# First weight loads as two half-megabyte transfers, layer-norm moments on ScalarE, and earlier row gathers, in a kernel bound by TensorE

## The chip, the cores and the metric

The kernel runs on one core of a Trainium2 chip. The metric is the device time of one execution in microseconds (us). On most chips the executions of one kernel agree within about 0.3%, with single ones about 1% off, so differences of 0.3% can be seen only with several runs of both kernels, taken on the same chip in alternating rounds. All runs told of here are undisturbed ("fast"). Every ratio is the mean time of one kernel's fast runs over the mean time of the kernel before in the same rounds, with a 95% interval; it is therefore not quite the ratio of the medians that stand beside it. "Same" means within 2%.

Engine names: PE is TensorE's matmuls, PEld its weight loads, DVE is VectorE, ACT is ScalarE, POOL is GpSimd, SP is SyncE, which here only issues transfers. All times inside a trace count from the start of the profiled span.

## The reference

The input x is 2048 rows of 512, in bfloat16. It is layer-normalized; one branch filters it in the frequency domain, the other is a gated MLP; the output is the sum of x and both branches.

```python
xn = _layernorm(x, axis=-1)                         # (1, 2048, 512)
# A: 2-D real FFT, times (w_r + 1j*w_i), inverse FFT
# B: with w_gate, w_up (512 x 1792) and w_down (1792 x 512)
g = jnp.einsum("bsd,df->bsf", xn, w_gate)
u = jnp.einsum("bsd,df->bsf", xn, w_up)
b = jnp.einsum("bsf,fd->bsd", gelu(g) * u, w_down)
return x + A(xn) + b
```

## The kernel before

A small list scheduler written into the kernel orders all operations; each has an engine, a duration, its dependencies and a priority. The rows of x are cut into 16 "columns" of 128 rows. The first four columns are transposed on TensorE, so that the gate and up matmuls can begin as soon as column 0 is normalized and the first slices of the weights are there. Later columns are transposed by transfers.

The loads, in the order of issue. The first two slices (128 columns each) of gate go on SP's queue, those of up on ScalarE's queue:

```python
    load_x(0, 1)                              # 128 KB
    d_ident = load_ct("ident", "ident", "ACT")
    load_x(1, 1)
    load_w(0, 2, ("SP", "ACT"))               # gate 256 KB on SP, up 256 KB on ScalarE's queue
    ...                                       # (a dummy GELU: loads ScalarE's table)
    load_x(2, 2)
    load_w(2, 4)
    load_w(4, 6)
    load_x(4, 4)
    load_w(6, 10)
    load_x(8, 4)
    load_w(10, 14)
```

Column 0 is transposed in two halves that share one PSUM buffer (the other columns in one piece); ScalarE copies the first half out, VectorE the second:

```python
    def pe_transpose(c, due):
        b = _Buf("S")                         # one buffer for the column
        ...
            o = pe(0.24 / n, mm, (XN[c][h], d_ident), due - 2, new=(b,) if h == 0 else (), use=(b,))
            XT[c].append((act, dve)[h](0.1 + 0.35 / n, ev, (o,), due - 30, use=(b,)))
```

The first matmul groups take column 0 alone, then column 1 alone, then pairs; and the six row gathers of the spectral weights wait for column 11 to be normalized:

```python
    FIRST = [(0, 1, 0, 4), (1, 1, 0, 4), (0, 2, 4, 2), (2, 2, 0, 2), (2, 2, 2, 2), (2, 2, 4, 2)]
    ...
    d_tw.append(dma(P * n * 2, lambda ...: gather(k, s, c, a, n), [g_idx] + XN[11], 20, eng="POOL", issue=1.2))
```

## Time and profile before

| what | before |
|---|---|
| time | 179.41 us (median of 3), later 179.33 (6 runs) |
| span of the profiled run | 177.6 us |
| TensorE busy | 173.4 us, 98% |
| first transpose | 5.78 us |
| first gate matmul | 6.89 us |
| first group of 512-wide gate matmuls (full pace) | 18.52 us |
| last matmul | 174.70 us |

The page of the kernel before, its busy times by engine and the chain of waits that ended last:

```profile
PE 173.4 (98%) x1100; PEld 92.9 (52%) x1100; DVE 118.1 (66%) x266; ACT 87.4 (49%) x158; POOL 18.6 (10%) x33
PE 91%; ACT 3%; DVE 3%; issue 1%; POOL 0%; DVEq 0%; POOLq 0%
```

TensorE is the bound. From 18.52 us to the last matmul it hardly waits; a change of the kind studied here can only shift that block to the left, by doing the first 18 us in less time. The timeline of PE in the kernel before; the columns are start, duration, engine, line, operation, output <- inputs, shape and count:

```profile
5.78 0.65 PE L428 MATMUL tp<-CT,xn 128*128 128x128 bf16 x4
6.23 0.63 PE L380 MATMUL warm<-warm 128*128 128x128 bf16 x4
6.89 0.82 PE L502 MATMUL g_ps<-xnT,Wg_sb 128*128 128x128 bf16 x8
7.55 0.61 PE L502 MATMUL u_ps<-xnT,Wu_sb 128*128 128x128 bf16 x8
...
18.52 1.03 PE L502 MATMUL g_ps<-xnT,Wg_sb 128*128 128x512 bf16 x4
```

`tp` are the transposes of column 0, `warm` are fillers, meant only to keep TensorE's clock up, `g_ps` and `u_ps` are gate and up. The first useful gate matmul comes 1.1 us after the first transpose. It needs the first half of column 0, which ScalarE copies from 6.47 to 6.84; VectorE's copy of the second half starts only after that, and holds up the third matmul. The timelines of ACT and DVE in the kernel before show both copies (the last column says what the engine sat idle for):

```profile
6.47 0.37 ACT L431 COPY xnT<-tp 128x256 bf16<-128x256 bf16 x1 [3.29 <-PE tp L428]
6.88 0.29 DVE L431 COPY xnT<-tp 128x256 bf16<-128x256 bf16 x1 [0.83 <-ACT xnT L431]
```

The view of the transfers issued in the first 2.5 us of the kernel before (queue, count, size of each, us from issue to landing): gate, issued at 1.65 us, lands at 5.85; up, issued at 1.12 on ScalarE's queue, at about 5.3.

```profile
Wu_sb<-in_B_w_up_dram ACTq DMA_DIRECT2D x1, 256.0 KB, 4.2
Wg_sb<-in_B_w_gate_dram SPq DMA_DIRECT2D x1, 256.0 KB, 4.2
```

### The profile page before, as it was taken

Reading aid. Unit: us, or ns where it says so; the run is one execution under the profiler, and the core shown is the slowest. Engines: PE = TensorE matmul, PEld = TensorE weight load, DVE = VectorE, ACT = ScalarE, POOL = GpSimd, SP = SyncE. Lnnn points to the kernel's source line nnn. Section 1 sums busy time; section 2 is a strip of 40 time slices with the busy share of each in tenths; the row PEclk is TensorE's granted clock in tenths of the full one; section 3 lists DMA queues with packets and bytes.
Section 4 is the critical chain, followed back from the end, with each engine's and each line's share of the span. In section 5 each row is a group of like instructions: output and inputs, shape, how many; then the busy total and the mean of one; then the engine's idle time right before and its main releaser. Section 6 shows DMA issues by size and latency. Waiting matters only on the chain.

```text
span 177.6 us, 3041 instructions
## 1 busy us (share of the span) xinstructions
PE 173.4 (98%) x1100; PEld 92.9 (52%) x1100; DVE 118.1 (66%) x266; ACT 87.4 (49%) x158; POOL 18.6 (10%) x33
## 2 busy tenths in 40 slices
PE   6999999999999999999999999999999999999993
PEld 2598545545554544554555455554445444544463
DVE  1869999999537995889999885336442541632522
ACT  3162437456789737999998855453111211211100
POOL 3212138743200000000000000000000000000000
PEclk9999999999999999999999999999999999999999
DMA  5999487999297001302211121100222221322212
GB/s 144 311 355 359 86 270 84 223 296 193 52 347 255 2 0 29 93 2 59 61 48 37 37 59 37 27 0 0 84 68 66 83 89 59 92 80 69 74 45 59
DMA packets 23182, 19.24 MB, mean 108 GB/s; under 512 B 8512, under 2 KB 21824, under 8 KB 23168
## 3 DMA queue, kind: packets, MB, share of 16 engines
q1 hardware_dynamic: 22176, 17.57, 35.0%
q0 software_dynamic: 320, 1.19, 3.1%
q10 hardware_dynamic: 672, 0.30, 0.6%
q8 instruction: 8, 0.13, 0.3%
q14 instruction: 6, 0.05, 0.1%
HBM read 13.28 MB, written 2.10 MB: 87 GB/s over the span
## 4 chain that ended last, share of the span: by engine, by line
PE 91%; ACT 3%; DVE 3%; issue 1%; POOL 0%; DVEq 0%; POOLq 0%
PE u_ps L502 25%; PE g_ps L502 25%; PE warm L380 3%; ACT E L652 2%; PE yp L818 2%; PE bp L581 2%; PE gp L767 2%; PE yp__2078 L872 2%; PE yp__1994 L872 2%; PE yp__1967 L872 2%; PE yp__1936 L872 2%; PE yp__1909 L872 2%; PE yp__1820 L872 2%; PE yp__1793 L872 2%; PE yp__1762 L872 2%; PE yp__1735 L872 2%
## 5 line engine op out<-in xcount | busy, mean ns | idle before, releaser
L502 PE MATMUL g_ps<-xnT,Wg_sb 128*128 128x512 bf16 (+2 forms) x264 | 58.1, 347 | 0.0
L502 PE MATMUL u_ps<-xnT,Wu_sb 128*128 128x512 bf16 (+2 forms) x264 | 57.9, 347 | 0.0
L527 DVE TENSOR_TENSOR hT<-u_ps,ge 128x512 bf16<-128x512 f32 x56 | 38.4, 685 | 17.5 <-PE u_ps L502 14.4
L519 ACT ACTIVATE ge<-g_ps 128x512 bf16<-128x512 f32 x56 | 33.5, 598 | 30.5 <-PE g_ps L502 26.5
L502 PEld LDWEIGHTS <-Wu_sb 128*128 128x128 bf16 x264 | 24.3, 98 | 22.3 <-DMA Wu_sb<-in_B_w_up_dram 0.2
L502 PEld LDWEIGHTS <-Wg_sb 128*128 128x128 bf16 x264 | 24.3, 98 | 20.7 <-issue 0.2
L872 PEld LDWEIGHTS <-hT 128*128 128x128 bf16 x252 | 23.0, 98 | 21.9
L824 ACT CAST yf<-yp 128x512 bf16<-128x512 f32 x16 | 9.3, 586 | 37.6 <-PE yp L818 37.6
L652 ACT CAST E<-ep 64x512 bf16<-64x512 f32 x32 | 18.5, 579 | 1.1 <-PE ep L646 0.7
L396 DVE BATCH_NORM_STATS2 st<-x_t 128x6 f32<-128x512 bf16 x16 | 10.5, 676 | 4.8 <-DMA x_t<-in_A_x_dram 4.8
L629 ACT CAST ds<-dp 128x512 bf16<-128x512 f32 x16 | 8.8, 589 | 1.1 <-PE dp L624 1.0
L773 ACT CAST Gs<-gp 128x512 bf16<-128x512 f32 x16 | 8.6, 593 | 1.0 <-PE gp L767 1.0
L406 POOL TENSOR_TENSOR rstd<-ve,half 128x2 f32<-128x2 f32 (+2 forms) x7 | 6.6, 949 | 21.9 <-DVE ve L404 21.9
L585 ACT CAST Bs<-bp 128x512 bf16<-128x512 f32 x16 | 8.3, 603 | 0.5 <-PE bp L581 0.5
L818 PEld LDWEIGHTS <-Gs 128*128 128x128 bf16 x64 | 4.8, 98 | 3.5
L380 PE MATMUL warm<-warm 128*128 128x512 bf16 (+1 forms) x14 | 5.1, 539 | 1.3 <-POOL half L373 1.3
L412 DVE TENSOR_SCALAR xn<-x_t,mv,rstd 128x512 bf16<-128x512 bf16 (+1 forms) x17 | 6.1, 399 | 0.3 <-POOL rstd L406 0.3
L818 PE MATMUL yp<-CT,Gs 128*128 128x128 bf16 x64 | 6.0, 219 | 0.0
L683 DVE TENSOR_TENSOR m<-X,TW 128x1024 bf16<-128x1024 bf16 x8 | 5.5, 692 | 0.2
L624 PEld LDWEIGHTS <-Bs 128*128 128x128 bf16 x64 | 4.4, 98 | 2.4
L689 DVE TENSOR_TENSOR m<-X,TW 128x1024 bf16<-128x1024 bf16 x8 | 5.5, 684 | 0.0
L646 PE MATMUL ep<-ds,CT 128*128 128x512 bf16 x16 | 5.4, 379 | 0.0
(103 smaller groups left out, 169.0 us busy)
## 6 DMA issues: line engine op xcount, KB each, us to landing
y<-in_A_x_dram SPq DMA_DIRECT2D x16, 128.0 KB, 2.1
F<-F SPq DMA_DIRECT2D x32, 64.0 KB, 2.0
out_dram<-y SPq DMA_DIRECT2D x15, 128.0 KB, 1.7
Wd_sb<-in_B_w_down_dram SPq DMA_DIRECT2D x2, 896.0 KB, 8.3
x_t<-in_A_x_dram SPq DMA_DIRECT2D x3, 512.0 KB, 6.8
Wg_sb<-in_B_w_gate_dram SPq DMA_DIRECT2D x2, 512.0 KB, 6.8
Wu_sb<-in_B_w_up_dram SPq DMA_DIRECT2D x2, 512.0 KB, 9.1
Wg_sb<-in_B_w_gate_dram SPq DMA_DIRECT2D x3, 256.0 KB, 5.1
```

The source lines that it names most:

```text
L380: nc.tensor.matmul(tiles["warm"][:, 0:w], lhsT=warm[:, 0:P], rhs=warm[:, 0:w], start=True, stop=True)
L396: V.bn_stats(out=st[:], in_=x_t[:, c])
L502: nc.tensor.matmul(tiles[f"{nm}.{key}"][:, f * w:f * w + w], lhsT=W[:, e, (f0 + f) * P:(f0 + f + 1) * P], rhs=rhs(e), start=(f + e == 0), ...
L519: nc.scalar.activation(out=e[:, 0:nf * w], in_=tiles[f"g_ps.{key}"][:, 0:nf * w], func=AF.Gelu_apprx_tanh)
L527: V.tensor_tensor(out=out, in0=tiles[f"u_ps.{key}"][:, 0:nf * w].rearrange("p (f w) -> p f w", w=w) if nf > 1 else tiles[f"u_ps.{key}"][:, ...
L585: nc.scalar.copy(out=o, in_=tiles[f"bp.{cg}.{q}"][:].rearrange("p c (r g a) -> p (c r) g a", r=2, a=4))
L629: nc.scalar.copy(out=ds[:].rearrange("p (s k t) -> p s k t", s=2, t=2), in_=tiles[f"dp.{G}"][:].rearrange("p s t k -> p s k t"))
L652: nc.scalar.copy(out=tiles[f"E.{g}"][64 * h:64 * h + 64, r], in_=tiles[f"ep.{g}.{h}"][64 * r:64 * r + 64])
L773: nc.scalar.copy(out=o, in_=tiles[f"gp.{g}.{h}"][:].rearrange("p q (n a) -> p (q n) a", a=4))
L818: nc.tensor.matmul(yp[:, q], lhsT=tiles["G"][:, q, c], rhs=IQ[q], start=(q == 0), stop=(q == 3), skip_group_check=True)
L824: nc.scalar.copy(out=tiles[f"yf.{c // 2}"][:, c % 2], in_=tiles[f"yp.{c}"][:])
L872: nc.tensor.matmul(y[:, s], lhsT=tiles[sb, f][:, cl * P:(cl + 1) * P], rhs=Wd_sb[:, f, s], start=(f == 0), stop=False)
```

## The change

The intent: the first weights come as two loads of four slices, gate then up, both on SP's queue, with rows of 1 KB instead of 512 B; ScalarE computes mean and variance of columns 1 and 3, so that column 1 is ready sooner and VectorE has less to do; each transposed half has a PSUM buffer of its own; the matmuls of a group use the first half of the contraction first; columns 2 and 3 go one by one; the gathers wait for column 3 only and so run between the weight loads. The core of the diff:

```diff
-    load_w(0, 2, ("SP", "ACT"))
+    load_w(0, 4)
     load_x(2, 2)
-    load_w(2, 4)
     load_w(4, 6)
...
+    def layernorm_act(c, due, halves, after=(), after2=()):
+        ...
+        s = act(0.62, lambda: moment(AF.Identity, scale=-1.0 / D, accum_out=sm[:, k:k + 1]), ...)
+        q = act(0.72, lambda: moment(AF.Square, bias=sm[:, k:k + 1], scale=1.0, accum_out=sm[:, k + 1:k + 2]), ...)
...
     def pe_transpose(c, due):
-        b = _Buf("S")
...
         for h in range(n):
+            b = _Buf("S")
...
-    layernorm(1, 1, -25, first)
...
+    layernorm_act(1, -25, 2)
...
+    layernorm(2, 1, -22, XN[1])
...
+    layernorm_act(3, -19, 1, XT[0], XT[1])
...
-                            [g_idx] + XN[11], 20, eng="POOL", issue=1.2))
+                            [g_idx] + XN[3], 20, eng="POOL", issue=1.2))
...
-            for f in range(a, b):
-                for e in range(NE):
+            for f, e in sorted(((f, e) for f in range(a, b) for e in range(NE)), key=lambda k: (k[1] // 2, k)):
...
-        step = min(nf, 2)
+        step = 4 if n == 1 else min(nf, 2)
...
-    FIRST = [(0, 1, 0, 4), (1, 1, 0, 4), (0, 2, 4, 2), (2, 2, 0, 2), (2, 2, 2, 2), (2, 2, 4, 2)]
+    FIRST = [(0, 1, 0, 4), (1, 1, 0, 4), (0, 2, 4, 2), (2, 1, 0, 4), (3, 1, 0, 4), (2, 2, 4, 2)]
```

The rest of the diff adjusts durations and delays that the scheduler believes, makes the statistics of columns 4 to 15 wait for column 3, and cuts the fillers after the first transposes from four to two.

The scheduler plans with the loads and the gathers, so an edit of either can also change the order of instructions on the engines.

More of the change, by code (lines that the diff above doesn't have):

```diff
@@ L172, in run @@
                         continue
-                    at = max([d.end + d.lag + self.HOP for d in o.deps if d.eng != "PE" or o.eng != "PE"] + [0.0])
+                    at = max([d.end + (0.0 if d.eng == o.eng and not d.nbytes else d.lag + self.HOP)
+                              for d in o.deps if d.eng != "PE" or o.eng != "PE"] + [0.0])
                     if o.nbytes and o.eng != "POOL" and len(lanes) >= 8:
@@ L265 @@
     eps = pc.tile([P, 2], F32, name="eps")
+    sm = pc.tile([P, 4], F32, name="sm")
     tiles = {}
@@ L314, in load_x @@
         q = nc.sync if eng == "SP" else nc.scalar
-        o = load(n * P * D * 2, lambda: q.dma_start(out=x_t[:, c0:c0 + n], in_=x_v[:, c0:c0 + n]), deps, eng=eng)
+        o = load(n * P * D * (1.9 if c0 > 1 else 1), lambda: q.dma_start(out=x_t[:, c0:c0 + n], in_=x_v[:, c0:c0 + n]), deps, eng=eng)
         for c in range(c0, c0 + n):
@@ L323, in load_w @@
             q = nc.sync if e == "SP" else nc.scalar
-            os.append(load(NE * P * P * 2 * (f1 - f0),
+            os.append(load(NE * P * P * (2.3 if f1 - f0 < 4 else 2.05) * (f1 - f0),
                            lambda t=t, v=v, q=q: q.dma_start(out=t[:, :, a:b], in_=v[:, :, a:b]), eng=e))
@@ L374 @@
     wb = _Buf("S")
-    NWARM, NGAP, GAP = 10, 1, 4
+    NWARM, NGAP, GAP = 10, 1, 2
     def warm_mm(w):
@@ L405, in layernorm, with moment, normalize @@
             out=ve[:, k], in0=mv[:, k, 1], scalar1=EPS, scalar2=None, op0=ALU.add), ag, due - 5)
+        normalize(c0, n, due, e, halves)
+    def layernorm_act(c, due, halves, after=(), after2=()):
+        k = 2 * (c // 2)
+        def moment(func, **kw):
+            nc.scalar.activation(out=xn[:, c], in_=x_t[:, c], func=func, **kw)
+        s = act(0.62, lambda: moment(AF.Identity, scale=-1.0 / D, accum_out=sm[:, k:k + 1]), [XD[c]] + list(after), due - 30)
+        q = act(0.72, lambda: moment(AF.Square, bias=sm[:, k:k + 1], scale=1.0, accum_out=sm[:, k + 1:k + 2]), [s] + list(after2), due - 30)
+        e = dve(0.07, lambda: V.tensor_scalar(
+            out=ve[:, c:c + 1], in0=sm[:, k + 1:k + 2], scalar1=1.0 / D, scalar2=EPS, op0=ALU.mult, op1=ALU.add), (q,), due - 9)
+        normalize(c, 1, due, e, halves, sm[:, k:k + 1], ALU.add)
+    def normalize(c0, n, due, e, halves, mean=None, op=ALU.subtract):
+        k = slice(c0, c0 + n)
         r = add("POOL", 0.55, lambda: nc.gpsimd.tensor_tensor(
@@ L412, in layernorm, with ev @@
                 XN[c].append(dve(0.04 + 0.29 / halves, lambda c=c, d=d: V.tensor_scalar(
-                    out=xn[:, c, d], in0=x_t[:, c, d], scalar1=mv[:, c, 0:1], scalar2=rstd[:, c:c + 1],
-                    op0=ALU.subtract, op1=ALU.mult), (r,), due - 2.5))
-        return ag
+                    out=xn[:, c, d], in0=x_t[:, c, d], scalar1=mv[:, c, 0:1] if mean is None else mean,
+                    scalar2=rstd[:, c:c + 1], op0=op, op1=ALU.mult), (r,), due - 2.5))
     def pe_transpose(c, due):
         XT[c] = []
-        b = _Buf("S")
         n = len(XN[c])
         for h in range(n):
+            b = _Buf("S")
             es = range(h * NE // n, (h + 1) * NE // n)
             def mm(h=h, es=es):
-                if h == 0:
-                    psum(f"tp.{c}", [P, NE, P], BF16)
+                psum(f"tp.{c}.{h}", [P, NE, P], BF16)
                 for e in es:
-                    nc.tensor.transpose(tiles[f"tp.{c}"][:, e], xn[:, c, e * P:(e + 1) * P], ident)
-            def ev(es=es, eng=(nc.scalar.copy, V.tensor_copy)[h]):
-                eng(out=xnT[c // 4][:, es[0]:es[-1] + 1, c % 4], in_=tiles[f"tp.{c}"][:, es[0]:es[-1] + 1])
-            o = pe(0.24 / n, mm, (XN[c][h], d_ident), due - 2, new=(b,) if h == 0 else (), use=(b,))
+                    nc.tensor.transpose(tiles[f"tp.{c}.{h}"][:, e], xn[:, c, e * P:(e + 1) * P], ident)
+            def ev(h=h, es=es, eng=(nc.scalar.copy, V.tensor_copy)[h]):
+                eng(out=xnT[c // 4][:, es[0]:es[-1] + 1, c % 4], in_=tiles[f"tp.{c}.{h}"][:, es[0]:es[-1] + 1])
+            o = pe(0.24 / n, mm, (XN[c][h], d_ident), due - 2, new=(b,))
             XT[c].append((act, dve)[h](0.1 + 0.35 / n, ev, (o,), due - 30, use=(b,)))
@@ L438, in dma_transpose @@
                     XN[c], due - 30, lag=1.0)]
-    first = layernorm(0, 1, -28, (), 2)
-    layernorm(1, 1, -25, first)
-    for c in range(4):
-        if c == 2:
-            layernorm(2, 2, -22, XT[0])
-        pe_transpose(c, -28 + 3 * c)
-        if c < NGAP:
-            dummies(GAP, -29.9 + 3 * c, XN[c], P)
+    layernorm(0, 1, -28, (), 2)
+    layernorm_act(1, -25, 2)
+    pe_transpose(0, -28)
+    dummies(GAP, -29.9, XN[0], P)
+    pe_transpose(1, -25)
+    layernorm(2, 1, -22, XN[1])
+    pe_transpose(2, -22)
+    layernorm_act(3, -19, 1, XT[0], XT[1])
+    pe_transpose(3, -19)
     for c0, n, due in ((4, 2, 14), (6, 2, 16), (8, 4, 24), (12, 4, 32)):
-        layernorm(c0, n, due)
+        layernorm(c0, n, due, XN[3])
         for c in range(c0, c0 + n):
@@ L499, in mm @@
                 psum(f"{nm}.{key}", [P, D], tag=tag)
-            for f in range(a, b):
-                for e in range(NE):
-                    nc.tensor.matmul(tiles[f"{nm}.{key}"][:, f * w:f * w + w], lhsT=W[:, e, (f0 + f) * P:(f0 + f + 1) * P],
-                                     rhs=rhs(e), start=(f + e == 0), stop=(f == nf - 1 and e == NE - 1),
-                                     skip_group_check=nf > 1)
+            for f, e in sorted(((f, e) for f in range(a, b) for e in range(NE)), key=lambda k: (k[1] // 2, k)):
+                nc.tensor.matmul(tiles[f"{nm}.{key}"][:, f * w:f * w + w], lhsT=W[:, e, (f0 + f) * P:(f0 + f + 1) * P],
+                                 rhs=rhs(e), start=(f + e == 0), stop=(f == nf - 1 and e == NE - 1),
+                                 skip_group_check=nf > 1)
         g = [o for c in range(c0, c0 + n) for o in XT[c]]
-        step = min(nf, 2)
+        step = 4 if n == 1 else min(nf, 2)
         us = []
```

## The prediction

> **What bounds the kernel now.** The page gives TensorE 98% of the span, and the chain of waits is TensorE for 91% of it. From 11.70 us to 174.93 us the chain is matmuls at full pace (0.86 us for four 128x512); the waits view shows no TensorE wait after the first loads. So only the start can give time.
>
> In the chain and timeline, warm-up matmuls fill 1.34 to 5.79. The first transpose (column 0) waits until 5.78 for the normalized half; the first gate matmul comes at 6.89. From there to 11.70 the useful work is 64 matmuls of 128 columns and 12 transposes: 76 x 0.056 = 4.23 us. Lost there, from the single matmul records: 0.21 us after the second gate matmul (the second half of column 0 is not yet copied; the VectorE copy starts at 6.88, only after the ScalarE copy that ran 6.47 to 6.84), and 0.17 us before 8.84 (PEld waits for Wu_sb). Between 5.79 and 6.89 four transposes and four fillers run at half pace (107 ns each).
>
> **What the change does.**
> - A PSUM buffer per transposed half: the ScalarE copy can start about 6.2 instead of 6.47, the VectorE copy about 6.47. The gate matmuls take all slices of half one first, so they can start near 6.6 and not stop for half two. Saves about 0.3 and 0.2 us.
> - Weights: kilobyte packets take 46 ns, 512 B packets 27 ns in the trace, so a megabyte takes about 3.0 us instead of 3.5. Gate (four slices) should land near 5.2 to 6, up near 6.7 to 7.4, needed only at 7.5. Saves 0.17 us.
> - Column 1 on ScalarE: the Trainium skill ("ScalarE: Activation LUTs", "What ACT_TABLE_LOAD costs") gives 186 ns + 0.833 ns per element, 93 ns more per pointer operand: estimate 0.61 and 0.71 us; the trace agrees roughly (copies of 128x512: 0.59). Moments done near 5.3, its transposes come near 6.5 instead of 8.0, partly in dead time: 0 to 0.2 us saved.
> - Columns 2 and 3 go separately, in 64 narrow matmuls instead of 32 of 256 columns: adds 0.07 us.
> - Row gathers (1.19 MB, six of 1 to 1.7 us on GpSimd) move from 27-36 us to about 11-18, among the weight loads, and delay rstd of columns 4 to 7. Weights 6 to 9 land near 14.5, needed near 18; columns 4 to 7 have about 7 us to spare. Off the chain: 0.
>
> The clock: the Trainium skill ("TensorE: Matmul & The Clock Gate", "Part 1: The HAM clock gate") says the array starts at half rate and is released after a busy window of 3413 ns, at a moment the kernel does not set. The trace agrees: 427 ns between dummies, 107 between fillers up to 6.55, 56 from 6.89 on. Work brought before about 6.8 runs at half pace, which takes back about 0.1 us.
>
> **Sum.** 0.3 + 0.2 + 0.17 + 0.1 - 0.07 - 0.1 = about 0.6 us of 179.4: predicted 178.8 us, range 178.1 to 179.5. Chances: faster by over 2%: 0.01; within 2%: 0.98; slower: 0.01.
>
> **What would show it.** First gate matmul near 6.6, no gap after it; the first 128x512 gate group about 18.0 instead of 18.5; from there the same chain, shifted by 0.6 us; gathers at 11 to 18 us with no TensorE wait.
>
> **What would make it wrong.** The up weights land later than 7.5, since they queue behind 0.5 MB of gate; gathers slow x or weight loads so that TensorE waits near 10 to 20 us; the clock is released a window later (up to 1.7 us worse); ScalarE's moments hold up the copy of column 0; the new instruction order makes new stalls in the middle, which has none now.

## The result and the profile after

The kernel after took 179.86 us (median of 6 runs, 179.59 to 180.43), the kernel before in the same rounds 179.33 (6 runs, 179.21 to 179.73). The ratio is 1.0032, interval 1.0011 to 1.0053. The class is "same", as predicted, but the sign is wrong: a loss of about 0.5 us instead of a gain of 0.6, and outside the predicted range.

The page of the kernel after, busy times by engine and chain of waits:

```profile
PE 171.7 (96%) x1112; PEld 92.8 (52%) x1130; DVE 118.5 (66%) x265; ACT 90.1 (51%) x166; POOL 17.1 (10%) x34
PE 93%; DMA 4%; issue 1%; SPq 1%; DVE 0%
```

A transfer is in the chain now, 4% of a span of 178.2 us. (PE's busy time is not to be compared closely: 1112 matmuls are recorded against 1130 weight loads, so some matmul records are missing, and regular gaps of 0.22 us in this trace are such holes.) The timeline of PE in the kernel after (its last line counts one matmul because the view's window ended at 19.2 us):

```profile
5.49 0.54 PE L443 MATMUL tp<-CT,xn 128*128 128x128 bf16 x4
5.87 0.28 PE L381 MATMUL warm<-warm 128*128 128x128 bf16 x2
7.29 1.07 PE L517 MATMUL g_ps<-xnT,Wg_sb 128*128 128x128 bf16 x16 [1.14 <-DMA Wg_sb<-in_B_w_gate_dram]
8.19 0.39 PE L443 MATMUL tp<-CT,xn 128*128 128x128 bf16 x4
8.80 1.07 PE L517 MATMUL u_ps<-xnT,Wu_sb 128*128 128x128 bf16 x16 [0.22 <-DMA Wu_sb<-in_B_w_up_dram]
...
19.00 0.38 PE L517 MATMUL g_ps<-xnT,Wg_sb 128*128 128x512 bf16 x1
```

The first transposes are 0.3 us earlier than before, yet the first gate matmul is 0.4 us later, because TensorE stands 1.14 us for the gate weights, and again for up. The first 512-wide group comes at 19.00 instead of 18.52; from there to the last matmul it is 156.14 us against 156.18. The whole loss of the profiled run that can be placed, 0.48 of 0.6 us, is in the first 19 us. The waits view of the kernel after (engine, output, line <- releaser: us in total, times, longest us), of which the kernel before has only one line of this kind, 0.2 us of PEld for up:

```profile
PEld L517 <- DMA Wg_sb<-in_B_w_gate_dram: 1.3, 1, 1.3
PE g_ps L517 <- DMA Wg_sb<-in_B_w_gate_dram: 1.1, 1, 1.1
PEld L517 <- DMA Wu_sb<-in_B_w_up_dram: 0.4, 1, 0.4
PE u_ps L517 <- DMA Wu_sb<-in_B_w_up_dram: 0.2, 1, 0.2
```

PEld and PE are two sides of one wait, not two. The view of the transfers issued in the first 2.5 us of the kernel after:

```profile
Wg_sb<-in_B_w_gate_dram SPq DMA_DIRECT2D x1, 512.0 KB, 5.6
Wu_sb<-in_B_w_up_dram SPq DMA_DIRECT2D x1, 512.0 KB, 6.6
```

Gate was issued at 1.65 us, as before, and landed at 7.25; up, issued at 2.12, landed at 8.75. The prediction had said 5.2 to 6 and 6.7 to 7.4. The chain in order of time of the kernel after begins, after the issue of the loads on SP, with just this transfer:

```profile
2.12 6.63 DMA Wu_sb<-in_B_w_up_dram
8.75 0.05 issue
8.80 1.07 PE u_ps L517 x16
```

What the change meant to do inside the core worked. The timelines of ACT and DVE in the kernel after show ScalarE's moments of column 1 and the two copies of column 0, which no longer wait for each other:

```profile
3.53 0.63 ACT L413 ACTIVATE xn<-x_t 128x512 bf16<-128x512 bf16 x1 [0.92 <-DMA x_t<-in_A_x_dram]
4.07 0.19 ACT L413 ACTIVATION_READ_ACCUMULATOR xn<-x_t 128x1 f32 x1
4.29 0.72 ACT L413 ACTIVATE xn<-x_t,sm 128x512 bf16<-128x512 bf16 x1
5.81 0.37 ACT L446 COPY xnT<-tp 128x256 bf16<-128x256 bf16 x1 [0.71 <-PE tp L443]
6.07 0.29 DVE L446 COPY xnT<-tp 128x256 bf16<-128x256 bf16 x1 [0.32 <-PE tp L443]
```

Both halves were copied by 6.36, so the gate matmuls could have begun near 6.3.

### Why the gate weights were late

The table counts the packets of 512 B or more that start on each queue in a quarter of a microsecond, from the packet records of the traces. Queue SP carries x and then gate; after its last packets of x (1 KB each) there is a stretch with almost nothing on it.

| us | before: SP / ScalarE | after: SP | gate on ScalarE's queue (a3 below): SP / ScalarE |
|---|---|---|---|
| 2.90 to 3.15 | 20 / 33 | 35 | 40 / 9 |
| 3.15 to 3.40 | 20 / 68 | 11 | 13 / 26 |
| 3.40 to 3.65 | 5 / 123 | 11 | 5 / 48 |
| 3.65 to 3.90 | 3 / 138 | 5 | 0 / 80 |
| 3.90 to 4.15 | 66 / 81 | 37 | 0 / 87 |
| 4.15 to 4.40 | 95 / 40 | 57 | 0 / 93 |

SP's third load, then, starts to flow only near 3.9 us in the kernel before too. But there the packets of up on ScalarE's queue fill that stretch; in the kernel after nothing does. In addition, seven 1 KB packets of SP's queue that start between 2.9 and 4 us in the kernel after take 0.5 to 1.29 us each, where such a packet usually takes 0.046. And a load is done only when all its parts are. The Trainium skill ("DMA: Bandwidth & Descriptors", "Why a DMA increments its semaphore by 16 and not by 1") says that each of the 16 DMA engines posts its own increment; the trace agrees, with 16 records of 4 bytes for each load. In the kernel after, 15 of gate's had been written by 5.86 us and the 16th not before 6.49. From the last such record to the landing it is some 0.4 us more (in run d4 below, 5.87 and 1.65 + 4.6 = 6.25). Run d4 also shows which of these matters more: there SP's queue had started its first 768 packets of 1 KB (256 of x and as many as gate has) at 5.34 us, against 5.50 in the kernel after, but the last part of gate was written at 5.87, against 6.49 or later. Most of the 1.0 us between these two landings is thus the last part, and not the stretch.

How full the transfer engines were can be read too. By the view of stretches of time the core moved, between 2.90 and 4.00 us, 64 GB/s in the kernel after, 242 in the kernel before and 238 in a3; between 4.00 and 7.20 it moved 351, 306 and 339 GB/s, with the 16 engines busy all the time. So the rate is no limit in the stretch, but it is one after it.

### The profile page after: what moved, and what is told of

Its sections match the earlier page's. It is cut to its first block, busy times and chain, and to the rows that moved or that the text cites. A ratio compares the mean times of both kernels' runs of the same rounds, so it can differ in the third digit from the quotient of the medians.

```text
span 178.2 us, 3088 instructions
## 1 busy us (share of the span) xinstructions
PE 171.7 (96%) x1112; PEld 92.8 (52%) x1130; DVE 118.5 (66%) x265; ACT 90.1 (51%) x166; POOL 17.1 (10%) x34
## 4 chain that ended last, share of the span: by engine, by line
PE 93%; DMA 4%; issue 1%; SPq 1%; DVE 0%
PE u_ps L517 27%; PE g_ps L517 26%; DMA Wu_sb<-in_B_w_up_dram 4%; PE bp L596 2%; PE gp L782 2%; PE yp L833 2%; PE dp L639 2%; PE ep L661 2%; PE yp__2111 L887 2%; PE yp__1969 L887 2%; PE yp__1911 L887 2%; PE yp__1826 L887 2%; PE yp__1795 L887 2%; PE yp__1739 L887 2%; PE yp__2058 L887 2%; PE yp__2027 L887 2%
## 5 line engine op out<-in xcount | busy, mean ns | idle before, releaser
L517 PE MATMUL u_ps<-xnT,Wu_sb 128*128 128x512 bf16 (+2 forms) x276 | 57.3, 336 | 0.5 <-DMA Wu_sb<-in_B_w_up_dram 0.2
L517 PE MATMUL g_ps<-xnT,Wg_sb 128*128 128x512 bf16 (+2 forms) x272 | 56.4, 335 | 1.4 <-DMA Wg_sb<-in_B_w_gate_dram 1.1
L667 ACT CAST E<-ep 64x512 bf16<-64x512 f32 x32 | 18.5, 579 | 1.8 <-PE ep L661 1.4
L397 DVE BATCH_NORM_STATS2 st<-x_t 128x6 f32<-128x512 bf16 x14 | 9.4, 673 | 3.8 <-DMA x_t<-in_A_x_dram 3.8
L423 POOL TENSOR_TENSOR rstd<-ve,half 128x1 f32<-128x1 f32 (+2 forms) x8 | 6.4, 809 | 23.9 <-DVE ve L405 23.1
L429 DVE TENSOR_SCALAR xn<-x_t,mv,rstd 128x512 bf16<-128x512 bf16 (+1 forms) x15 | 5.4, 406 | 1.6 <-POOL rstd L423 1.6
L381 PE MATMUL warm<-warm 128*128 128x512 bf16 (+1 forms) x12 | 4.4, 533 | 1.3 <-POOL half L374 1.3
L782 PEld LDWEIGHTS <-F 128*128 128x128 bf16 x64 | 4.2, 98 | 1.9
```

The source lines that it names most:

```text
L397: V.bn_stats(out=st[:], in_=x_t[:, c])
L517: nc.tensor.matmul(tiles[f"{nm}.{key}"][:, f * w:f * w + w], lhsT=W[:, e, (f0 + f) * P:(f0 + f + 1) * P], rhs=rhs(e), start=(f + e == 0), ...
L667: nc.scalar.copy(out=tiles[f"E.{g}"][64 * h:64 * h + 64, r], in_=tiles[f"ep.{g}.{h}"][64 * r:64 * r + 64])
```

## The experiments

The theory: the new order and size of the first loads costs the time, and the rest of the change gains. Its rivals: the gathers among the weight loads cost it, or ScalarE's moments and the new order of the instructions do. Eighteen runs were made: eleven new kernels, six of these or the kernel after once more, and the kernel of a6 under the name d4. Each gave the reference's result.

### a1 and a2: the loads alone, undone and done

a1 is the kernel after with the loads and the `step` of before:

```diff
-    load_w(0, 4)
+    load_w(0, 2, ("SP", "ACT"))
     load_x(2, 2)
+    load_w(2, 4)
...
-        step = 4 if n == 1 else min(nf, 2)
+        step = min(nf, 2)
```

> The changed kernel with the first weights loaded as before (two slices in 512-byte rows, the first up slices on the other queue, the next two slices after x) and the gate and up matmuls again two slices at a time; all the rest of the change stays. Theory L (the loss is the late landing of the first four-slice gate and up loads: 7.2 and 8.75 us): first gate matmul near 6.3 to 6.6 us, no TensorE wait over 0.3 us after it, total 178.7 to 179.0, faster than before by 0.2 to 0.4%. Rival R (the loss is from the gathers, the ScalarE moments or the new instruction order): 179.7 to 180.0, slower than before as the changed kernel is.

a2 is the kernel before with only the loads of after (the reverse edit, without the change of `step`).

> The kernel before with only the new loads (gate then up, four slices each, on one queue). Theory L: the first gate matmul waits for the weights until 7.0 to 7.4 and the up matmul until about 8.7, total 179.9 to 180.6. Rival R: within 0.15% of before, 179.1 to 179.6.

Before took 179.31 (11 runs). a1 took 178.98, ratio 0.9991 (0.9950 to 1.0031; one of its six runs at 181.0 widens it): no wait for weights, and these two lines in its timeline of PE:

```profile
6.74 0.61 PE L518 MATMUL g_ps<-xnT,Wg_sb 128*128 128x128 bf16 x8
18.36 1.03 PE L518 MATMUL g_ps<-xnT,Wg_sb 128*128 128x512 bf16 x3
```

So gate was used at 6.74, and the first 512-wide group came at 18.36. a2 took 181.22, ratio 1.0108 (1.0088 to 1.0128), clearly slower. The edit of the loads alone cost the kernel before 1.9 us, more than a2's expectation had (179.9 to 180.6) and more than the whole change lost. The waits view of a2 shows why it is more:

```profile
PE g_ps L501 <- ACT xnT L430: 0.8, 1, 0.8
PEld L501 <- DMA Wu_sb<-in_B_w_up_dram: 0.6, 1, 0.6
PE u_ps L501 <- DMA Wu_sb<-in_B_w_up_dram: 0.5, 1, 0.5
```

Beside the wait for up there is one, at 14.9 us, for the transposed columns 2 and 3. Their x, issued at 2.69 behind the megabyte of weights, was waited for until 8.67. What held them after that is in a2's chain: the scheduler, planning with the new loads, had put VectorE's statistics of column 4 before the normalization of columns 2 and 3, and these stood until 11.65 for the x of columns 4 to 7, issued at 4.68. So a part of the 1.9 us is this new order. Gate itself was not late in a2: its first gate matmul came at 6.68, where 7.0 to 7.4 had been expected. In a1 too the order changed on VectorE and ScalarE, and `step` with it. a3, below, is the clean test: it moves one load and leaves the order on every compute engine as it was.

### a3 and a4: one of the two loads on ScalarE's queue

The order of all instructions is kept; only the first gate load (a3) or the first up load (a4) is issued on ScalarE's queue right after the identity matrix, at 1.12 us.

```diff
-    load_w(0, 4)
+    load_w(0, 4, ("ACT", "SP"))        # a4: ("SP", "ACT")
...
     order = plan.run()
+    order.remove(WD[0][0])             # a4: WD[0][1]
+    order.insert(order.index(d_ident) + 1, WD[0][0])
```

> The changed kernel, same instruction order on every compute engine, but the four-slice gate load is issued on the ScalarE queue right after ident (about 1.1 us); up stays on the first queue. Theory L, with the cause that 3.0 to 4.0 us is a hole in the transfers because nothing else is in flight while the gate load starts up: gate lands near 5.3 to 6.0, up near 7.0 to 7.6, first gate matmul near 6.4, total 178.6 to 179.0. If the four-slice loads are slow as such (kilobyte rows or size, whatever the queue): gate still lands near 7, total 179.6 to 180.0. Rival R: unchanged, 179.7 to 180.0.

> The changed kernel, same order, but the four-slice up load is on the ScalarE queue (as in the kernel before) and gate on the first. Theory L: up fills the hole and lands near 5.5 to 6.5, but gate shares the engines with it and lands near 7 to 7.5: the first gate matmul comes no earlier than 6.9, the wait for up (8.75) is gone; total 179.2 to 179.6, between the changed kernel and a3. Rival R: unchanged, 179.7 to 180.0.

a3 took 179.28, ratio 0.9990 (0.9965 to 1.0015); a4 179.50, ratio 1.0003 (0.9986 to 1.0021). The first gate matmul and the transfer of up in a3, from its timeline of PE and its view of transfers:

```profile
6.77 1.22 PE L517 MATMUL g_ps<-xnT,Wg_sb 128*128 128x128 bf16 x16
Wu_sb<-in_B_w_up_dram SPq DMA_DIRECT2D x1, 512.0 KB, 5.6
```

In a3 gate landed at 1.12 + 4.7 = 5.8 us, and there is no wait for weights at all; the first 512-wide group came at 18.29, against 19.00. (The time is nevertheless above the expected 178.6 to 179.0; in this trace column 0 was ready late, with the first transpose at 5.91.) Up, now SP's third load, took the 5.6 us that gate had taken. In a4 gate took 5.6 again, though the other 512 KB had left its queue, and the wait of 0.9 us stayed:

```profile
7.28 1.07 PE L517 MATMUL g_ps<-xnT,Wg_sb 128*128 128x128 bf16 x16 [0.92 <-DMA Wg_sb<-in_B_w_gate_dram]
```

So in both kernels the load on ScalarE's queue landed at 5.7 to 5.8 and the one on SP's queue, behind x, at 7.25. This doesn't separate the place on the queue from the bytes that go before: in a4 the core moved 374 GB/s between 4.00 and 4.60 us with all 16 engines busy, nearly all of it up, and SP's third load began only at 4.60. In a4 up was there early (5.7), which took the second wait away, and the 512-wide group came at 18.60.

The Trainium skill ("DMA: Bandwidth & Descriptors", "Rules for kernel authors") says that spreading transfers over issuing engines doesn't help bandwidth and only saves issue time. Here gate landed 1.43 us sooner (7.25 to 5.8); 0.53 of that is the earlier issue (1.65 to 1.12), the other 0.9 is a shorter time from issue to landing. In this stretch, where SP's queue started few packets, the second queue gave more than issue time: 238 GB/s instead of 64 between 2.90 and 4.00 us.

### b1, b2, a5, a6: on a chip where the kernel before varied more

These four ran together on a chip where the kernel before took 180.03 (179.45 to 181.77), a wide spread. b1 splits the first gate and up loads into two halves of the contraction, which is what the first matmuls use first; b2 does the same and puts gate's first half on ScalarE's queue.

```diff
+            for h in range(2 if f0 == 0 else 1):
+                q = nc.scalar if f0 + h == 0 and t is Wg_sb else nc.sync      # b2 only
+                es = slice(2 * h, 2 * h + 2) if f0 == 0 else slice(0, NE)
-                           lambda t=t, v=v, q=q: q.dma_start(out=t[:, :, a:b], in_=v[:, :, a:b]), eng=e))
+                               lambda ...: q.dma_start(out=t[:, es, a:b], in_=v[:, es, a:b]), eng="SP"))
...
+    order.remove(WD[0][2])                                                    # b2 only
+    order.insert(order.index(d_ident) + 1, WD[0][2])
```

> The changed kernel, same instruction order on every compute engine and same queue, but the first gate and up loads are each cut in two loads of 256 KB by the contraction halves (still kilobyte rows), which is the order in which the matmuls use them. If size is the cause (a matmul that needs 256 KB waits for a 512 KB load): the first half lands near 6.0 to 6.3, the first gate matmul comes at 6.2 to 6.5, up near 8.0 to 8.3, total 179.0 to 179.4. If the slow start of the load after x on this queue is the cause, whatever its size: first gate matmul still after 6.8, total 179.5 to 180.0.

> As b1, with the first gate half on the ScalarE queue right after ident (256 KB there, as much as the kernel before had of up). Theory L: it lands near 5.3, the first gate matmul waits for column 0 only (6.3 to 6.8), the rest of gate lands by 7.0 and up by 8.0 with no TensorE wait over 0.2 us; total 178.5 to 178.9, faster than before by 0.2 to 0.45%. Rival R: 179.6 to 180.0.

a5 is a1 with the moments of columns 1 and 3 back on VectorE:

```diff
-    layernorm_act(1, -25, 2)
+    layernorm(1, 1, -25, (), 2)
-    layernorm_act(3, -19, 1, XT[0], XT[1])
+    layernorm(3, 1, -19, XT[1])
```

> The kernel of a1 (old loads, which take the late weights away) with columns 1 and 3 normalized from VectorE statistics again. If the ScalarE moments gain what was forecast (0 to 0.2 us): first 128x512 gate group 0 to 0.2 us later than in a1 (18.36), total 178.9 to 179.2. If they hurt: earlier than in a1, total under 178.8.

a6 is the kernel after with the gathers late, as before:

```diff
-                            [g_idx] + XN[3], 20, eng="POOL", issue=1.2))
+                            [g_idx] + XN[11], 20, eng="POOL", issue=1.2))
```

> The changed kernel with the row gathers after column 11 again, as before; same order on TensorE and ScalarE. Theory L: no effect on the critical path, total within 0.15% of the changed kernel (179.6 to 180.1), first gate matmul still near 7.2, up near 8.7. Rival R (gathers among the weight loads cost the time): 179.3 or less.

b1 took 181.80, ratio 1.0075; b2 180.92, 1.0033 (0.9989 to 1.0077); a5 180.88, 1.0034 (0.9992 to 1.0077); a6 181.25, 1.0058 (1.0016 to 1.0099). In their first 19 us b1, b2 and a6 did what was hoped: b1's gate matmuls began at 6.46, b2's at 6.24, and the 512-wide group came at 18.45 and 18.26; a6 still waited 0.7 us for gate and came to it at 18.42. a5's profiled run, the longest of its seven (182.99), came to that group only at 21.44, after a row of waits from 17 us on. In the others the time was lost later, in waits of 0.6 to 1.5 us between 18 and 36 us, of which another chip showed the like only in c3 and c4 (0.7 and 0.97, below). In a6, TensorE waited 1.5 us at 34.3 for VectorE, which itself stood still for 1.47 us with no wait for x. I don't know what this chip did there. The call decides nothing on sizes below 1%, and so b2, a1, a5 and the kernel after were run once more elsewhere.

### c1 to c4: the same kernels once more

c1 is the kernel after, c2 is a1, c3 is a5, c4 is b2, all unchanged. Before took 179.40 (179.16 to 179.59).

> The changed kernel itself, so that the three others of this call have it on the same chip. Theory L: 0.1 to 0.5% slower than before; gate load landing 5.2 to 5.7 us after its issue, up 6.3 to 6.8 after its issue, first 128x512 gate group 18.4 to 19.0. The last call ran on a chip whose kernel before was slower and more spread (180.03, 179.45 to 181.77), and its waits from 19 to 36 us are not understood; if this call runs on such a chip, the same waits should show in all four.

> The kernel of a1 (old loads, all the rest changed). Theory L: 0.4 to 0.8 us faster than c1; against before 0.1 to 0.4% faster. Rival R: equal to c1 within 0.2 us.

> The kernel of a5 (old loads, columns 1 and 3 from VectorE statistics). If the ScalarE moments are worth what was forecast: 0 to 0.2 us slower than c2. If they cost: faster than c2 by over 0.1 us.

> The kernel of b2 (first gate half on the ScalarE queue). Theory L: first 128x512 gate group 18.1 to 18.3, fastest of the four: 0.5 to 1.0 us faster than c1, 0.2 to 0.45% faster than before. Rival R: equal to c1 within 0.2 us.

c1 took 179.94, ratio 1.0026 (1.0013 to 1.0039): the loss of the kernel after is real. Its waits view repeats the cause:

```profile
PE g_ps L517 <- DMA Wg_sb<-in_B_w_gate_dram: 1.2, 1, 1.2
PE u_ps L517 <- DMA Wu_sb<-in_B_w_up_dram: 0.2, 1, 0.2
```

Gate again took 5.6 us to land, and the 512-wide group came at 19.04. c2 took 179.15, ratio 0.9987 (0.9968 to 1.0006); c3 179.38, 0.9996 (0.9983 to 1.0009); c4 179.37, 0.9997 (0.9974 to 1.0019). ScalarE's moments are thus worth 0.2 us at most in the medians, and the intervals of c2 and c3 overlap: no effect can be claimed.

c2, c3 and c4 came to the 512-wide group at 18.33, 18.16 and 18.12, earlier than the 18.52 of before, but their profiled runs were the longest of each (180.02, 179.89 and 180.29) and lost it again. The timeline of DVE in c2:

```profile
19.66 0.69 DVE L398 BATCH_NORM_STATS2 st<-x_t 128x6 f32<-128x512 bf16 x1 [1.22 <-DMA x_t<-in_A_x_dram]
```

The x of columns 8 to 11, issued at 8.2 us, landed at 19.65, against 17.3 in the kernel before and 18.5 in a1's good trace. VectorE has almost no idle time in c2 from 14 to 45 us except this, so it is late for the folds of the spectral branch, and TensorE waits for those: 0.28, 0.36 and 0.37 us between 27.7 and 42.6 us. c4 showed the same with columns 12 to 15 (landing 30.8 us, VectorE idle for 1.1 us, a TensorE gap of 0.97 us at 34.2). That the landing of x decides this is read from the traces; that the early gathers make it late was still only a theory.

### d1 to d4: the gathers

d1 is a1, d2 is b2, d4 is the kernel after, each with late gathers (the edit of a6). d3 is the opposite: the kernel before with early gathers and no other edit. In d2 and d4 only GpSimd's own order changes with it; in d1 and d3 the scheduler also moved a few of VectorE's instructions (some eight of 266 in d3).

```diff
-                            [g_idx] + XN[11], 20, eng="POOL", issue=1.2))
+                            [g_idx] + XN[3], 20, eng="POOL", issue=1.2))
```

> The kernel of a1 (old loads) with the row gathers after column 11 again, as in the kernel before. Theory G (the early gathers delay x of columns 8 to 15, VectorE, which is busy without a break from 14 to 45 us, waits for them and hands the delay to TensorE's fold matmuls): x of columns 8 to 11 lands by 17.8 (18.5 in a1, 19.65 in its repeat), no VectorE wait for x after 12 us, no TensorE wait over 0.3 us from 20 to 50, total 178.5 to 178.9 in every run, spread under 0.5 us. Rival N (the waits from 20 to 50 us are chip noise or come from the new instruction order): spread as in a1 and its repeat (178.5 to 181.0).

> The kernel of b2 (first gate half on the ScalarE queue) with late gathers. Theory G: first 128x512 gate group 18.1 to 18.3 and no later waits over 0.3 us: 178.4 to 178.8, faster than before by 0.3 to 0.5%. Rival N: 178.8 to 180.3 as in its repeat.

> The kernel before with the early gathers alone (order on TensorE and ScalarE the same as before). Theory G: x of columns 8 to 11 lands 1 to 2 us later than the 17.3 of before, VectorE waits for it in some runs, total 179.4 to 180.4 with a spread over 0.5 us. Rival N: as before, 179.2 to 179.6.

> The changed kernel with late gathers (a6 again, on this call's chip). Its start is as late as the changed kernel's (gate and up waits stay, first 128x512 gate group near 19.0), so with either theory 179.6 to 180.0; with theory G no VectorE wait for x after 14 us.

Before took 179.43 (179.01 to 180.12). d3 took 180.32, ratio 1.0056 (1.0028 to 1.0083): the early gathers, with the order that the scheduler then made, cost the kernel before about 0.9 us. Its profiled run, at 179.88 one of the faster ones, shows the gathers between 9.8 and 19.7 us instead of 27.4 to 35.6, and these waits, the second in place of 4.8 us in two waits before:

```profile
PEld L502 <- DMA Wu_sb<-in_B_w_up_dram: 0.5, 1, 0.5
DVE st L396 <- DMA x_t<-in_A_x_dram: 5.2, 3, 3.3
```

The 512-wide group is at 18.65 and the time from there to the last matmul 156.55, 0.37 more than before. The wait for up, at 8.97 us, comes before the first gather (9.84), so it can't be put down to the gathers; the later part can, or to VectorE's new order. This trace explains 0.5 us of the cost, in a run that was only 0.45 us above before; the slower runs have no trace.

d1 took 179.45, ratio 1.0000 (0.9976 to 1.0023): in a1 late gathers bring nothing (0.9991 and 0.9987 with early ones). Its x of column 0 happened to land late, with the first transpose at 6.22 us instead of 5.58 to 6.00, which hides a gain of some tenths if there was one. But the theory had also given a spread under 0.5 us, and the six runs went from 178.85 to 179.86: for a1 it failed. d2 took 179.04, ratio 0.9978 (0.9958 to 0.9998), VectorE has no wait for columns 8 to 11 there, and it is the first kernel to beat before, though by less than expected (178.4 to 178.8). d4 took 179.36, ratio 1.0013 (0.9984 to 1.0043), better than its expectation (179.6 to 180.0); in its trace gate landed after 4.6 us instead of 5.6.

### e1 and e2: once more

e1 is d4 again, e2 is d2 again. Before took 179.49 (179.40 to 180.15, 11 runs).

> The kernel after the change with its row gathers made late, unchanged, a second time. In its first run the gate weights happened to land early (first gate matmul at 6.5 us instead of 7.3) and it took 179.36. If late gathers themselves make the first weights land early: first gate matmul again at 6.4 to 6.8 us, time within 0.2 of before. If the early landing was chance and the gathers act only later in the span: first gate matmul at 7.2 to 7.4 us, first 512-wide gate group near 19.0, time 0.2 to 0.5 above before.

> The best version of the earlier runs, a second time: gate's first half on ScalarE's queue, late gathers, the new ScalarE moments. If its gain is real: 0.2 to 0.5 us below before (ratio 0.997 to 0.999), first 512-wide gate group near 18.1, no wait of VectorE for x of columns 8 to 11. If it was chance of the run: within 0.1 of before or above it.

e2 took 179.09 (178.82 to 179.58), ratio 0.9971 (0.9954 to 0.9988). Together with d2 this is settled: this version is 0.4 us faster than before, and by the medians of different calls about 0.8 us faster than the kernel after. The first gate matmuls and the first 512-wide group in e2's timeline of PE:

```profile
6.39 1.05 PE L520 MATMUL g_ps<-xnT,Wg_sb 128*128 128x128 bf16 x16
18.14 1.03 PE L520 MATMUL g_ps<-xnT,Wg_sb 128*128 128x512 bf16 x4
```

e1 took 180.05 (179.25 to 181.48), ratio 1.0053 (1.0021 to 1.0084). Its two slowest runs had a granted clock of 0.99, all others 0.998 or more; the three runs at a clock of 1.0 average 179.70. Yet its profiled run, the fastest (179.25), shows what the change does when gate lands early:

```profile
6.46 1.21 PE L517 MATMUL g_ps<-xnT,Wg_sb 128*128 128x128 bf16 x16
18.00 1.03 PE L517 MATMUL g_ps<-xnT,Wg_sb 128*128 128x512 bf16 x4
```

So the two expectations for e1 each came half true: gate was early in the trace (4.5 us to land), and the time was nevertheless above before. Only a trace shows where gate landed, and there is one trace per kernel.

| kernel with the change's order of loads | gathers | gate's landing after issue | records of gate's parts: 15th / 16th | first gate matmul | 512-wide group |
|---|---|---|---|---|---|
| after | early | 5.6 us | 5.86 / 6.49 or later | 7.29 | 19.00 |
| c1 | early | 5.6 us | 6.13 / 6.45 or later | 7.31 | 19.04 |
| a6 | late | about 5.1 us | 6.26 / 6.28 | 6.80 | 18.42 |
| d4 | late | 4.6 us | 5.84 / 5.87 | 6.51 | 18.15 |
| e1 | late | 4.5 us | 5.60 / 5.76 | 6.46 | 18.00 |

(a6's landing is taken from its first gate matmul, which waited for it.) The instructions on SP and the transfers up to this point are the same in all five; the gathers themselves are issued 6 us later, at 12.4 us or after 24 us. That gate landed early in all three with late gathers and late in both with early ones is therefore chance, an effect of the chip (c1 ran on another than a6, d4 and e1, which ran on three) or one of the gathers that I can't name. a2, whose gathers are late too, also had gate in time (6.68). What the kernel after does with gate at 4.5 us and early gathers was not seen.

## Why the prediction was right or wrong

- **TensorE bounds the kernel, and only the start can give time: right.** From the first 512-wide group to the last matmul after and before differ by 0.04 us in their profiled runs.
- **The two PSUM buffers and the new order of matmuls, worth 0.3 and 0.2 us: right as a mechanism, and visible where the weights are there.** In the kernel after the copies ended at 6.36. In e1 the first gate matmul came at 6.46 (predicted 6.6) and the 512-wide group at 18.00 (predicted 18.0). That the numbers meet so well is partly luck: the first transpose was 0.2 us earlier in e1 than before (5.58 against 5.78). From it to the first gate matmul it was 0.88 us against 1.11.
- **"Gate (four slices) should land near 5.2 to 6, up near 6.7 to 7.4", a gain of 0.17 us: this step failed.** In its place TensorE stood for 1.14 us and then for 0.22 us, and full pace came 0.48 us later than before instead of 0.5 earlier; gate landed at 7.25, up at 8.75. The estimate added up packet times, a megabyte in 3.0 us. It left out three things that the traces show: SP's third load starts to flow only near 3.9 us, in the kernel before as well; single packets of that stretch take up to 1.29 us and the load is not done before the slowest of its 16 parts; and the first matmul had needed 256 KB and now needs 512. How much each of the three costs is not separated, beyond the comparison with d4 above. With the loads of before (a1) or with gate on ScalarE's queue (a3) the wait is gone and so is the loss. The prediction's list of what could make it wrong named up, which was the smaller wait, and not gate.
- **"Off the chain: 0" for the gathers: wrong in one setting, not decided in others.** In the kernel after and in c1 the traces show no cost: x of columns 8 to 11 landed at 17.0 us, VectorE did not wait for it, and from the first 512-wide group to the last matmul it was 156.14 and 156.08 us. In the kernel before they cost 0.9 us (d3), together with the order that the scheduler made of them. With b2's loads late gathers went with 0.9978 and 0.9971 against 0.9997 and 1.0033, though in different calls. With a1's loads they made no difference, and with the change's own loads the runs do not agree (a6 and e1 slower than before, d4 about equal). The slack that the prediction counted, 7 us for columns 4 to 7, was there; where a cost was read from a trace (c2, c3, c4), it came from x of columns 8 to 15, through VectorE.
- **ScalarE's moments, 0 to 0.2 us: right within what can be seen** (c2 against c3). The two instructions took 0.63 and 0.72 us; the prediction's estimate from the skill's page was 0.61 and 0.71. Two more instructions of 0.19 us that read the accumulator were not foreseen; they did not delay the copy of column 0.
- **The clock.** "Takes back about 0.1 us" rested on a release at 6.55 to 6.9 us. In the kernel after the first transposes already ran at full pace, 56 ns apart, at 5.5. The Trainium skill ("TensorE: Matmul & The Clock Gate", "Part 1: The HAM clock gate") says that the moment varies by 500 ns from run to run; the traces show more: in two traces of one kernel, whose first filler is at 1.34 us in both, matmuls were 0.06 us apart from 6.00 us on (a1) and still 0.11 apart at 7.1 (c2). A term of this size can't be predicted, and the times of single traces in the first 19 us carry some of it.
- **x of column 0** was used 0.3 us earlier in the kernel after, which the prediction did not have. It is not shown to be an effect of the change: with the loads of before the first transpose came at 5.58 (c2, d3), 5.78, 6.00 and 6.22 us in different runs, with those of after at 5.41 to 5.66.

What stays open: why gate's landing varies by 1.1 us between runs of the same loads, whether late gathers or the chip have a part in that, whether the change with gate in time would be faster than before (d4 and e1 had it in their traces, and were about equal and slower by their means), and what one chip did between 18 and 36 us.

## What to carry to other kernels

At the start of a kernel ask when the first bytes that the first matmul needs have all landed, not when their packets could have passed: here a larger load with longer rows, whose packets take less time per byte (46 ns for 1 KB against 27 for 512 B), released its reader later. Put the first operand of the critical engine in a small load at the head of a queue of its own; here the best kernel (d2 and e2) has half of gate on ScalarE's queue, still in rows of 1 KB, and late gathers. And work taken off the critical engine's start can be lost on an engine with no slack further on: before moving transfers forward, look for the engine that would pass their delay on (here VectorE, through x of columns 8 to 15).

## What the Trainium skill lacked or had wrong

- "DMA: Bandwidth & Descriptors", "Anatomy of one DMA — SWDGE (gpsimd) path", fits the time of one transfer as 2.0 us plus its bytes over 436 GB/s; for 512 KB that is an estimate of 3.2 us. It is given for another path, and no page has one for a load that stands third on SP's queue: here 4.5 to 5.6 us from issue to landing, and 4.6 to 4.7 on ScalarE's queue behind 32 KB.
- The same page, "Rules for kernel authors", says that using a second issuing engine only saves issue time. At the start of this kernel it also shortened the time from issue to landing, from 5.6 to 4.7 us, and in the kernel after SP's queue started only 27 packets between 3.15 and 3.90 us, a stretch that the other queue's packets filled in a3. No page tells of such a stretch.
- No page has how far the 16 parts of one load can lie apart: 15 of gate's were recorded within 0.73 us (5.13 to 5.86) and the last at least 0.63 us later, in the kernel after. A single packet of 1 KB took up to 1.29 us, where 0.046 is usual.
- "ScalarE: Activation LUTs", "What ACT_TABLE_LOAD costs", has the time of an ACTIVATE right (0.61 and 0.71 us estimated, 0.63 and 0.72 measured) but does not say that one with an accumulator output is followed by an instruction that reads it, 0.19 us each.
- "TensorE: Matmul & The Clock Gate", "Part 1: The HAM clock gate", has the transition vary by 500 ns either way from run to run. Two traces of one kernel were over 1.1 us apart: full pace from 6.00 us on in a1, half pace until 7.1 in c2, with the same start of the fillers.
